# Forming the combine products of a mixture-of-experts layer among the first experts instead of in the output stage

## The chip, the cores and the metric

One core of one Trainium2 chip runs the kernel. The metric is the device time of one execution in microseconds (us). The kernel before takes 350.67 us, the median of three runs (350.11 to 351.55).

## What is computed

Causal attention over 2 batches, 12 heads, 448 positions and head size 64 gives x, 896 tokens of 768 numbers. Two layers follow, cut here to what matters:

```python
logits = x @ phi                       # 32 slots
slot_input = softmax(logits, 0).T @ x  # 8 experts of 4 slots
slot_out[e] = relu(slot_input[e] @ w1[e]) @ w2[e]
c = softmax(logits, 1)                 # combine weights, 896 x 32
y = c @ slot_out                       # never formed by the kernel
out = ((y @ w_a) * (y @ w_b)) @ w_out  # d_ff = 1536
```

With A = slot_out @ w_a and B = slot_out @ w_b (32 rows each), the product (y @ w_a) * (y @ w_b) is a sum over pairs of slots (i, j) of c_i c_j times A_i B_j. So the kernel forms two things for each of the 528 pairs of slots: the products c_i c_j for every token (called cc here), and the rows M = (A_i B_j + A_j B_i) @ w_out. The output is cc times M. The pairs are cut into five blocks, k = 0 to 4; blocks 0 to 3 hold 128 pairs, the last one 16.

## The kernel before, in words

The kernel issues every instruction in an order written out by hand (`manual_schedule`): each engine works its own list from the front, and waits there.

Attention fills the first 120 us. Meanwhile `w_a`, `w_b` and `w_out` arrive as packed halves (the `raw` tiles, 0 to 35, 768 KB each) and are turned into floats by `conv_begin` and `conv_step` (two ACT passes L174 and L177, one DVE pass L218). Raw 32 to 35 are the last four parts of `w_out`.

Then come the eight experts, whose weights stream through SyncE's queue as 64 tiles w0 to w63 of 768 KB, in the order of use. `order` (L456 to L480) gives each transfer its place and its home, one of the slots r0 to r3, q0 to q3, t0 to t3; `pump` (L486) issues transfers from the front of that list as long as the next one's slot is free, and stops at the first that is not. After the first two rounds over twelve slots (`HOMES`) the homes repeat over six slots, r0 to r3, q0 and q1 (`ring6`): a tile is then requested when the tile six places earlier has been used. `rsel`, a 320 KB table of zeros and ones that picks pairs of slots, is loaded after w31 (`NSEL`), and raw 32 to 35 stand after w21, w31, w32 and w33 (`RPOS`).

`group` runs the experts in `GROUPS` (0 to 3, then 4 and 5, then 6 and 7): for each expert `exp_h` (four tiles of first-layer weights, lines L682), `exp_hp`, and `exp_so` (four tiles of second-layer weights, L723). Between tiles `spare()` takes units of other work, as many as the table `BG` tells. In the first group these are the units that turn the softmax of the logits into `cst`, the transposed combine weights in two parts (`combine_units`: `cw_max`, `cw_copy`, `cw_turn`). In experts 2 and 3 (`KEEPE`) each tile is preceded by five small matmuls whose result nobody reads (`keep`, L354). In groups 1 and 2 the spare units are a `Stage`: `fold_a`, `fold_b`, `ab_chunk` (A and B of the slots just done, L809), `ab_turn`, the products A_i B_j on DVE (`products`, L891 to L903; `p_tile`, L922 and L923), the splitting of `w_out` into a high and a low part (`w_split`, ACT L947 then DVE L948, into `wtm` in slots t2, t3, and q0, q1 at the end), and the matmuls `m_mats` (L953) that give M for block 0 or 1.

The last stage (from 264 us) computes A and B for the last group (`half_chunk`, L839), M for blocks 2, 3 and 4 (`m_late`, L953), splits the remaining `w_out` (`w_late`), and forms cc. Its units sit in the gaps between PE's blocks (`gap`, with the table `TAIL`). Each `cc_step(n, k)` (L1111) takes 256 tokens and two of the five blocks: up to four selection matmuls pick c_i and c_j (L1134, two PSUM tiles), ACT copies the one (L1138), DVE multiplies by the other (L1139), ACT rounds the product to the high part (L1142), and POOL subtracts to get the low part (L1143). The narrow last block takes L1147 and L1149. `o_mats` (L1246, L1253) multiplies cc by M for 128 tokens at a time, and `o_store` evicts and stores.

Of the kernel before, what the change touches and what calls it, by code (L numbers as in the profile page):

```python
# [21 lines left out]
S = 448  # L22
# [7 lines left out]
for _i in range(7):  # L30
# [42 lines left out]
BG = {  # L73
# [24 lines left out]
KEEPE = (2, 3)  # L98
# [5 lines left out]
def moe_kernel(ctx: ExitStack, tc: tile.TileContext, pk, vt, phi, w1, w2, wab, wo, rsel, out):  # L104
# [16 lines left out]
    ident16 = const.tile([128, 128], BF16, name="ident16")  # L121
# [26 lines left out]
    phi_sb = const.tile([128, NPAIR, NSLOT], F32, name="phi_sb")  # L148
# [203 lines left out]
    def keep(ps, n):  # L352
        for _ in range(n):
            nc.tensor.matmul(  # L354
                ps, lhsT=ident16[:, 0:ps.shape[0]], rhs=ident16[:, 0:ps.shape[1]], start=True, stop=True,
                skip_group_check=True,
            )
# [97 lines left out]
    ring6 = ["r0", "r1", "r2", "r3", "q0", "q1"]  # L455
# [60 lines left out]
    def arrive(k):  # L516
        while cursor[0] < pos["w", k]:
# [3 lines left out]
            elif kind == "rsel":  # L521
                rr = slot_tile("q3", F32R, "rs")[0:64, 0:1280]
                nc.scalar.activation(out=rr, in_=rin[0], func=AF.Copy)
                mq[1] = rr.rearrange("p (k q j) -> p k q j", k=5, q=2)
                freed.add(("rsel", 0))
# [6 lines left out]
    with tc.manual_schedule():  # L532
# [216 lines left out]
        cst = r2.tile([64, 2, S], F32R, name="cst")  # L749
# [42 lines left out]

        def combine_units():
# [569 lines left out]
```

## Time and profile before

| | |
|---|---|
| median of three runs | 350.67 us |
| profiled execution, its own time | 351.46 us |
| its span, first to last instruction | 349.40 us |
| PE busy | 329.3 us (94%) |
| DVE busy | 207.8 us (59%) |
| ACT busy | 184.7 us (53%) |
| POOL busy | 83.7 us (24%) |
| DMA, mean over the span | 259 GB/s |

Busy is the time in which an engine ran an instruction. All times in the rows below are us from the start of the span. The profiled execution is 0.8 us above the median, 0.2%.

### The profile page before, as it was taken

How to read it: one execution, taken by the hardware profiler on the slowest of the kernel's cores; microseconds unless marked ns; L12 is line 12 of the kernel's file. 1: busy time of each engine (PE TensorE's matmuls, PEld its weight loads, DVE VectorE, ACT ScalarE, POOL GpSimd, SP SyncE). 2: the span in 40 equal slices, each digit the busy share in tenths (PEclk: the TensorE clock that was granted, in tenths of full speed). 3: DMA queues.
4: the chain of work that ended last, by engine and by line, in shares of the span. 5: the costliest groups of instructions: out<-in, count | busy, mean ns of one | idle time of the engine just before them, and what ended most of it. 6: DMA issues, size and time to landing. Idle time of an engine off the chain costs nothing.

```text
span 349.4 us, 7132 instructions
## 1 busy us (share of the span) xinstructions
PE 329.3 (94%) x2695; PEld 209.2 (60%) x2695; DVE 207.8 (59%) x587; ACT 184.7 (53%) x419; POOL 83.7 (24%) x150
## 2 busy tenths in 40 slices
PE   7999899999999989889988699998999999999996
PEld 5566556655656744433432357434565589989895
DVE  4799889979899640210034976408855899523221
ACT  2799989999899510131038344414445542543321
POOL 2566677765575300010000000000000000121210
PEclk9999999999999999999989989999999999999999
DMA  7799998998998889999999989779910000002122
GB/s 271 312 337 336 357 337 256 374 386 316 386 345 293 277 357 347 421 416 413 402 310 398 419 270 358 253 280 312 421 80 2 1 3 0 2 0 90 55 82 90
DMA packets 20225, 90.53 MB, mean 259 GB/s; under 512 B 2336, under 2 KB 5024, under 8 KB 20192
## 3 DMA queue, kind: packets, MB, share of 16 engines
q1 hardware_dynamic: 20192, 90.09, 69.2%
q8 instruction: 21, 0.34, 0.4%
q14 instruction: 12, 0.10, 0.1%
HBM read 87.33 MB, written 2.75 MB: 258 GB/s over the span
## 4 chain that ended last, share of the span: by engine, by line
PE 72%; DVE 12%; DMA 8%; ACT 4%; issue 1%; POOL 1%; SPq 1%; ACTq 0%; DVEq 0%; POOLq 0%
PE M L953 12%; PE s L277 10%; PE o L1253 9%; PE v L371 7%; PE t L335 6%; PE h L682 5%; PE so L723 5%; DMA qk<-in_pk_dram 4%; DMA raw<-in_wo_dram 4%; PE ab L809 3%; DVE pf L892 2%; DVE pt L891 2%; PE c L1134 2%; PE hp L702 2%; DVE pf L903 2%; PE xt L384 1%
## 5 line engine op out<-in xcount | busy, mean ns | idle before, releaser
L322 POOL TENSOR_SCALAR p<-p,rc 128x448 f32<-128x448 f32 (+6 forms) x84 | 59.0, 718 | 10.9 <-DVE rc L319 10.2
L277 PE MATMUL s<-qk 64*64 64x448 f32 (+6 forms) x336 | 47.2, 394 | 1.6 <-POOL qk L258 1.1
L1143 POOL TENSOR_TENSOR cc<-gt,cc 128x512 fp32r<-128x512 f32 (+1 forms) x6 | 6.6, 1101 | 165.3 <-ACT cc L1142 165.3
L298 ACT ACTIVATE p<-s,nm 128x448 f32<-128x448 f32 (+6 forms) x84 | 39.7, 484 | 8.9 <-DVE nm L288 8.2
L953 PE MATMUL M<-wt,P_t 128*128 128x384 f32 x168 | 35.7, 355 | 3.0 <-DVE wt L948 1.0
L953 PEld LDWEIGHTS M<-wt,P_t 128*128 128x128 f32 x168 | 29.2, 193 | 12.2 <-ACT wt L947 4.8
L283 DVE TENSOR_REDUCE nm<-s 128x1 f32<-128x448 f32 (+6 forms) x84 | 31.8, 413 | 6.2 <-PE s L277 6.2
L277 PEld LDWEIGHTS s<-qk 64*64 64x64 f32 x336 | 19.6, 133 | 22.0 <-issue 15.0
L682 PE MATMUL h<-w,sT 128*32 128x512 f32 x192 | 29.9, 613 | 2.1 <-ACT hs L695 1.6
L335 PE MATMUL t<-ident,p 128*128 128x128 f32 x192 | 31.1, 286 | 0.0
L948 DVE TENSOR_TENSOR wt<-wo,wt 128x384 fp32r<-128x384 f32 x48 | 23.8, 551 | 10.4 <-ACT wt L947 10.4
L947 ACT ACTIVATE wt<-wo 128x384 fp32r<-128x384 f32 x48 | 21.8, 513 | 13.6 <-PE M L953 13.1
L371 PE MATMUL v<-pT,v 128*64 128x192 f32 (+2 forms) x336 | 27.4, 299 | 0.0
L335 PEld LDWEIGHTS t<-ident,p 128*128 128x128 f32 x192 | 20.1, 141 | 11.4 <-issue 7.1
L723 PE MATMUL so<-w,hpad 128*32 128x384 f32 x256 | 24.8, 493 | 1.3 <-DMA w<-in_w_dram 0.6
L174 ACT ACTIVATE wab<-raw,shr 128x768 f32<-128x768 int8 x24 | 24.6, 1025 | 1.0 <-DMA raw<-in_wab_dram 1.0
L218 DVE SCALAR_TENSOR_TENSOR wab<-raw,wab 128x768 uint32<-128x768 uint32 x24 | 24.0, 1001 | 1.0 <-ACT wab L177 0.9
L177 ACT ACTIVATE wab<-wab,shr 128x768 int32<-128x768 f32 x24 | 22.9, 952 | 0.0
L371 PEld LDWEIGHTS v<-pT,v 128*64 128x64 f32 (+1 forms) x336 | 19.2, 135 | 6.0 <-issue 2.8
L1139 DVE TENSOR_TENSOR gt<-gt,c 128x512 f32<-128x512 f32 (+2 forms) x12 | 6.5, 544 | 25.7 <-ACT gt L1138 25.7
L809 PE MATMUL ab<-wab,sT 128*32 128x384 f32 x192 | 20.0, 523 | 0.5 <-DVE sT L647 0.5
L174 ACT ACTIVATE wo<-raw,shr 128x768 f32<-128x768 int8 x12 | 12.4, 1032 | 14.9 <-DMA raw<-in_wo_dram 14.9
(164 smaller groups left out, 533.5 us busy)
## 6 DMA issues: line engine op xcount, KB each, us to landing
w<-in_w_dram SPq DMA_DIRECT2D x64, 768.0 KB, 8.6
raw<-in_wab_dram SPq DMA_DIRECT2D x24, 768.0 KB, 6.7
raw<-in_wo_dram SPq DMA_DIRECT2D x12, 768.0 KB, 6.8
qk<-in_pk_dram SPq DMA_DIRECT2D x12, 448.0 KB, 6.2
v<-in_pk_dram SPq DMA_DIRECT2D x12, 192.0 KB, 6.3
out_dram<-ost SPq DMA_DIRECT2D x6, 384.0 KB, 2.3
v<-in_vt_dram SPq DMA_DIRECT2D x12, 32.0 KB, 6.1
out_dram<-ost SPq DMA_DIRECT2D x2, 192.0 KB, 1.9
```

The source lines that it names most:

```text
L174: nc.scalar.activation(out=dst, in_=top, func=AF.Prelu, bias=shr[:, 0:1], scale=1.0, alpha=2.0 ** -40)
L277: nc.tensor.matmul(sb[r, o:o + n], lhsT=qT[r, 64 * i:64 * i + 64], rhs=kT[r, 0:n], start=False, stop=True, skip_group_check=True,)
L283: nc.vector.tensor_reduce(out=d["nm"][:, c:c + 1], in_=sb[:, o:o + 64 * (i + 1)], axis=AX.X, op=ALU.max, negate=True)
L298: nc.scalar.activation(out=d["p"][:, POFF[i]:POFF[i] + n], in_=sb[:, o:o + n], func=AF.Exp, bias=d["nm"][:, c:c + 1], scale=d["scale"], ac ...
L322: nc.gpsimd.tensor_scalar(out=p[:, POFF[i]:POFF[i] + n], in0=p[:, POFF[i]:POFF[i] + n], scalar1=rc[:, CIX[i]:CIX[i] + 1], scalar2=1.0, op0 ...
L335: nc.tensor.transpose(ps[:, j, :], d["p"][:, o:o + 128], ident)
L371: nc.tensor.matmul(ps[r, 64 * i:64 * (i + n)], lhsT=v[k, kt, h, :], rhs=d["pT"][k, b0:b0 + by * (n - 1) + 1:by, r], start=(kt == 0), stop= ...
L682: nc.tensor.matmul(ps[32 * g:32 * g + 32, :], lhsT=sT[:, 0, c, :], rhs=wt[8 * e + i // 3][:, 512 * (i % 3):512 * (i % 3) + 512], start=(i ...
L723: nc.tensor.matmul(so[32 * g:32 * g + 32, 0:384], lhsT=t[:, c, :], rhs=wt[8 * e + 4 + i // 4][:, 384 * (i % 4):384 * (i % 4) + 384], start ...
L809: nc.tensor.matmul(abps[q][32 * g:32 * g + 32, 0:384], lhsT=sT[:, 1, c, :], rhs=w[:, c % 2, 384 * g:384 * g + 384], start=(c == 0), stop=( ...
L953: nc.tensor.matmul(mps[k][h][:, 0:384], lhsT=l[:, f, :], rhs=r, start=(n == 0 and i == 0), stop=(n == 11 and i == 2))
L1253: nc.tensor.matmul(ops[t][h][:, 0:384], lhsT=hl[k // 2][:, l, k % 2, o], rhs=mhl[k][:, r, 384 * h:384 * h + 384], start=(k == 0 and i == 0 ...
```

## The change

The selection matmuls, the ACT copy and the DVE product move from the last stage into the first group of experts, as ten new units `cc_make(n, k)` at the end of `combine_units`. They work on 512 tokens (n = 0) or 384 (n = 1) and one block k each, so there are 20 matmuls in place of 40. The products wait in memory: in slots q1 and q3 and in the places of the logits (`lsb`), of `phi` and of the softmax (`cs`). In the last stage `cc_split(n, k)` only rounds the high part (ACT) and subtracts for the low part (DVE, where POOL did it).

To make room, q1 and q3 leave the rotation after one use and q2 after one use and `rs`; `HOMES` has nine slots in its later rounds, and the steady ring has five (r0 to r3, q0). `rsel` comes after w11 in three transfers, is converted by three ACT copies as the first spare unit (`rs_cast`), and raw 32 moves to after w31. Two of the last stage's split parts of `w_out` move to later gaps and other slots (`w_late`, `TAIL["W"]`), the filler matmuls in experts 2 and 3 are gone (`KEEPE = ()`), and the scratch of block 4 moves from `lsb` to the place of `cst`.

```diff
-RPOS = (21, 31, 32, 33)
-NSEL = 31
+RPOS = (31,31,32,33)
+NSEL = 11
 HOMES = (
-    "r0", "r1", "r2", "r3", "q0", "q1", "q2", "q3", "t0", "t1", "t2", "t3", "r0", "r1", "r2", "r3", "q0", "q1",
-    "q2", "q3", "t0", "t1", "t2", "t3",
+    "r0", "r1", "r2", "r3", "q0", "q1", "q2", "q3", "t0", "t1", "t2", "t3", "r0", "r1", "r2", "r3", "q0", "t0", "t1", "t2", "t3", "r0", "r1", "r2", "r3", "q0", "t0", "t1", "t2", "t3",
 )
-NQ = 62
+NQ = 60
 BG = {
-    "B": ((0, 0, 0, 0, 0, 0, 0, 0, 0, 0, 0, 1, 0, 3, 0, 3, 3, 1, 0, 2), ...
+    "B": ((0, 0, 0, 0, 0, 0, 0, 0, 1, 1, 0, 0, 0, 1, 0, 1, 3, 1, 2, 1, 1, 0, 1, 1, 1, 0, 1, 1, 1, 0, 1, 1, 1, 0, 1), ...
 TAIL = {
-    "W": {2: 2, 3: 2, 4: 4, 13: 2, 14: 2, 15: 2, 16: 2},
+    "W": {2: 2, 3: 2, 4: 2, 13: 2, 14: 2, 15: 2, 16: 2, 18: 2},
-    "C": {36: 1, 39: 1, 41: 1, 43: 1, 46: 1, 49: 1, 53: 1, 56: 1, 59: 1, 62: 1, 65: 1, 68: 1},
+    "C": {30: 1, 32: 1, 34: 1, 36: 1, 38: 1, 40: 1, 42: 1, 44: 1, 46: 1, 48: 1},
-KEEPE = (2, 3)
+KEEPE = ()
...
-    ring6 = ["r0", "r1", "r2", "r3", "q0", "q1"]
+    steady = ["r0", "r1", "r2", "r3", "q0"]
...
-                home = ring6[nb % 6]
+                home = steady[nb % 5]
...
-                rin.append(slot_tile(s, F32, "rin")[0:64, 0:1280])
-                nc.sync.dma_start(out=rin[0], in_=rsel)
+                r2 = r2box["q"]
+                rin.append(r2.tile([128, 768], F32, tag="abt", bufs=1, name="rin0")[0:64])
+                for i in range(2):
+                    rin.append(r2.tile([128, 384], F32, tag="pt", bufs=2, name=f"rin{i + 1}")[0:64, 0:256])
+                for i in range(3):
+                    nc.sync.dma_start(out=rin[i], in_=rsel[:, (0, 768, 1024)[i]:(768, 1024, 1280)[i]])
...
+        def cc_make(n, k):
+            if not gs:
+                g_homes()
+            t0 = 512 * n
+            w = (512, 384)[n]
+            cstf = cst.rearrange("p b t -> p (b t)")
+            ab = []
+            for q in range(2):
+                ps = psM.tile([128, 512], F32, tag="m", name=f"c{q}_{n}_{k}")
+                ab.append(ps[:, 0:w])
+                nc.tensor.matmul(ab[q], lhsT=mq[1][:, k, q, :], rhs=cstf[:, t0:t0 + w], start=True, stop=True)
+            for i, g in enumerate(gs[n, k] if isinstance(gs[n, k], list) else [gs[n, k]]):
+                x = slice(256 * i, 256 * i + g.shape[-1])
+                nc.scalar.activation(out=g, in_=ab[0][:, x], func=AF.Copy)
+                nc.vector.tensor_tensor(out=g, in0=g, in1=ab[1][:, x], op=ALU.mult)
+
+        def rs_cast():
+            rr = slot_tile("q2", F32R, "rs")[0:64, 0:1280]
+            for i in range(3):
+                nc.scalar.activation(out=rr[:, (0, 768, 1024)[i]:(768, 1024, 1280)[i]], in_=rin[i], func=AF.Copy)
+            mq[1] = rr.rearrange("p (k q j) -> p k q j", k=5, q=2)
+
         def combine_units():
-            q = [cw_max, lambda: (cw_copy(0), cw_copy(1))]
+            q = [rs_cast, cw_max, lambda: (cw_copy(0), cw_copy(1))]
             for i in range(8):
                 q.append(lambda i=i: (cw_turn(i), i < 6 and cw_copy(i + 2)))
+            q += [lambda n=n, k=k: cc_make(n, k) for n in range(2) for k in range(5)]
...
-                    name = f"q{f - 8}" if self.k == len(STAGES) - 1 and f in (8, 9) else f"t{2 + f % 2}"
+                    name = {8: "q0", 11: "r0"}.get(f) if self.k == len(STAGES) - 1 else None
+                    name = name or f"t{2 + f % 2}"
...
         def late_next():
-            if wl_j[0] < (8 if nchunk[0] < 2 else 12 if nchunk[0] < 4 else 16):
+            if wl_j[0] < (6 if nchunk[0] < 2 else 10 if nchunk[0] < 4 else 16):
...
+        def cc_split(n, k):
+            if (n, k) in ((0, 0), (1, 2)):
+                cc_homes(n)
+            if k < 4:
+                h, l = ccv[n, k]
+                g = gs[n, k]
                 nc.scalar.activation(out=h, in_=g, func=AF.Copy)
-                nc.gpsimd.tensor_tensor(
-                    out=hl[k][:, 1, :, 0:w], in0=g, in1=h.bitcast(F32), op=ALU.subtract
-                )
+                nc.vector.tensor_tensor(out=l, in0=g, in1=h.bitcast(F32), op=ALU.subtract)
+                return
```

## Rows read from the trace of the kernel before

**Rows 1.** Windows: stretch, length, busy us (instructions) by engine, PEclk, DMA share, GB/s
```profile
132.60:164.70 32.10, 29.02 (x263) 12.45 (x263) 3.81 (x12) 5.51 (x10) 1.91 (x9) 1.00 1.01 415
175.30:200.00 24.70, 19.97 (x157) 8.02 (x153) 13.93 (x56) 13.63 (x22) 0.00 (x0) 0.93 1.01 378
307.00:346.00 39.00, 38.91 (x214) 35.26 (x212) 11.33 (x23) 12.89 (x28) 7.21 (x7) 1.00 0.17 66
```
**Rows 2.** Chain of waits from 296.0 to the end (53.4 us): shares, one piece
```profile
by line: PE o L1253 58.1%; PE M L953 17.7%; PE c L1134 12.8%; PE o L1246 5.0%; ACT ost L1266 0.9%; issue 0.1%; ACTq L1266 0.1%
...
303.79 0.67 PE c L1134 x4
```
**Rows 3.** Timeline of one cc step: start, us, engine, line, [idle before]
```profile
313.98 0.60 ACT L1138 ACTIVATE gt<-c 128x512 f32<-128x512 f32 x1 [2.01 <-PE c L1134]
...
314.61 0.69 DVE L1139 TENSOR_TENSOR gt<-gt,c 128x512 f32<-128x512 f32 x1 [3.30 <-ACT gt L1138]
...
315.33 0.64 ACT L1142 ACTIVATE cc<-gt 128x512 fp32r<-128x512 f32 x1 [0.75 <-DVE gt L1139]
...
316.04 1.28 POOL L1143 TENSOR_TENSOR cc<-gt,cc 128x512 fp32r<-128x512 f32 x1 [2.71 <-ACT cc L1142]
```
**Rows 4.** PE's timeline around expert 2's first tile and the last tile of expert 3
```profile
157.85 0.45 PE L354 MATMUL idle<-ident 128*128 128x128 bf16 x5
158.23 1.06 PE L682 MATMUL h<-w,sT 128*32 128x512 f32 x6
...
174.50 0.85 PE L723 MATMUL so<-w,hpad 128*32 128x384 f32 x8 [0.61 <-DMA w<-in_w_dram]
```
**Rows 5.** Transfers by tile, one issue each: rsel, then w32
```profile
L501 SPq DMA_DIRECT2D rin<-in_rsel_dram x1: 472/472/472, 166.8 to 166.8; - x1
...
DMA to landing us min/median/max: 13.3/13.3/13.3
...
L505 SPq DMA_DIRECT2D w<-in_w_dram x1: 334/334/334, 169.1 to 169.1; - x1
...
DMA to landing us min/median/max: 12.6/12.6/12.6
```
**Rows 6.** Windows (columns as Rows 1) around two transfers' stretches and two low-clock stretches
```profile
130.50:133.00 2.50, 2.08 (x25) 1.48 (x26) 1.03 (x3) 0.00 (x0) 0.00 (x0) 1.00 0.49 88
...
173.60:179.60 6.00, 4.26 (x35) 1.81 (x37) 1.87 (x3) 1.76 (x2) 0.00 (x0) 0.79 1.03 246
...
177.03:180.44 3.41, 3.07 (x20) 0.99 (x24) 1.86 (x3) 2.18 (x3) 0.00 (x0) 0.50 1.00 290
200.92:204.33 3.41, 3.41 (x11) 1.75 (x12) 3.06 (x14) 0.94 (x2) 0.00 (x0) 0.50 0.73 221
```
**Rows 7.** ACT's timeline: conversion of raw 34 at the start of group 1
```profile
183.62 1.04 ACT L174 ACTIVATE wo<-raw,shr 128x768 f32<-128x768 int8 x1 [2.14 <-DMA raw<-in_wo_dram]
```
**Rows 8.** Transfers issued at 235.2 and 236.7 (w55 and w56 of the kernel before)
```profile
L505 SPq DMA_DIRECT2D w<-in_w_dram x1: 328/328/328, 235.2 to 235.2; - x1
...
DMA to landing us min/median/max: 4.5/4.5/4.5
...
L505 SPq DMA_DIRECT2D w<-in_w_dram x1: 327/327/327, 236.7 to 236.7; - x1
...
DMA to landing us min/median/max: 6.8/6.8/6.8
```
**Rows 9.** PE's and DVE's timelines in expert 7 and stage 1
```profile
238.17 2.78 PE L682 MATMUL h<-w,sT 128*32 128x512 f32 x24 [0.70 <-ACT hs L695]
...
244.57 1.69 PE L723 MATMUL so<-w,hpad 128*32 128x384 f32 x16 [0.43 <-ACT wt L947]
...
246.44 1.96 DVE L948 TENSOR_TENSOR wt<-wo,wt 128x384 fp32r<-128x384 f32 x4
```
**Rows 10.** DVE's timeline before block 2's second products, and PE's wait for them
```profile
277.16 3.89 DVE L948 TENSOR_TENSOR whl<-wo,whl 128x384 fp32r<-128x384 f32 x8
...
284.83 3.22 PE L953 MATMUL M<-whl,P_t 128*128 128x384 f32 x17 [0.32 <-DVE P_t L923]
```

More of the change, by code (lines that the diff above doesn't have):

```diff
@@ L354, in keep @@
             nc.tensor.matmul(
-                ps, lhsT=ident16[:, 0:ps.shape[0]], rhs=ident16[:, 0:ps.shape[1]], start=True, stop=True,
-                skip_group_check=True,
+                ps, lhsT=ident.bitcast(BF16)[:, 0:ps.shape[0]], rhs=ident.bitcast(BF16)[:, 0:ps.shape[1]],
+                start=True, stop=True, skip_group_check=True,
             )
@@ L469, in moe_kernel @@
             if kind == "rsel":
-                order.append((kind, 0, "t2"))
+                order.append((kind, 0, "-"))
                 continue
@@ L489, in pump @@
             x, s = order[0][:2], order[0][2]
-            if s in holder and holder[s] not in freed:
+            if s == "-" and r2box.get("q") is None or s in holder and holder[s] not in freed and s != "-":
                 return
@@ L520, in arrive @@
                 conv_to(i)
[L521 to L525, printed above, removed]
             cursor[0] += 1
@@ L747, in group @@
                 spare()
-        cst = r2.tile([64, 2, S], F32R, name="cst")
+        cst = r2.tile([128, 2, S], F32R, tag="cst", bufs=1, name="cst")[0:64]
         cw = {}
@@ L1017, in p4_make @@
         def p4_make():
-            mx["p"] = const.tile([128, 12, 32], F32, tag="lsb", name="p4")
+            mx["p"] = r2.tile([128, 12, 32], F32, tag="cst", bufs=1, name="p4")
             nc.gpsimd.memset(mx["p"][:, :, 16:32], 0.0)
@@ L1033, in m4_copy @@
         def m4_copy():
-            mx["c"] = const.tile([128, 768], F32, tag="lsb", name="mc")
+            mx["c"] = r2.tile([128, 768], F32, tag="cst", bufs=1, name="mc")
             for h in range(2):
@@ L1076, in moe_kernel @@
                 mq[0] = slot_tile("q2", F32, "mq")
+                abl.append(r2.tile([128, 12, 2, NSLOT], F32, tag="abt", bufs=1, name="abt"))
+                av += [abl[0][:, :, q, :] for q in range(2)]
             if gi:
@@ new lines, in moe_kernel, with cc_homes @@
+        ccv = {}
+        def cc_homes(n):
+            if n == 0:
+                t3 = wabp.tile([128, 3, 2, 512], F32R, tag="wab3", bufs=1, name="cc3")
+                t4 = wabp.tile([128, 3072], F32R, tag="wab4", bufs=1, name="cc4")
+                for k in range(3):
+                    ccv[0, k] = t3[:, k, 0], t3[:, k, 1]
+                ccv[0, 3] = t4[:, 0:512], t4[:, 512:1024]
+                ccv[0, 4] = t4[:, 1024:1536],
+                for k in range(2):
+                    ccv[1, k] = [t4[:, 1536 + 768 * k + 384 * i:1920 + 768 * k + 384 * i] for i in range(2)]
+            else:
+                t = [slot_tile(j, F32R, f"cc{j}") for j in ("t0", "t1")]
+                for k in range(2):
+                    ccv[1, 2 + k] = [t[k][:, 384 * i:384 * i + 384] for i in range(2)]
+                ccv[1, 4] = t[0][:, 768:1152],
@@ L1148, in cc_step @@
                 q = slice(64, 96)
-                nc.vector.tensor_tensor(
-                    out=last[q, 0:w], in0=g[q, 0], in1=last[q, 0:w].bitcast(F32), op=ALU.subtract
-                )
+                nc.vector.tensor_tensor(out=last[q, x], in0=g[q], in1=last[q, x].bitcast(F32), op=ALU.subtract)
         mhl = {}
@@ L1169, in m_split @@
                 )
-        ccq = [(n, k) for n in range(4) for k in range(3)]
+        ccq = [(n, k) for n in range(2) for k in range(5)]
         ptq = {2: [0], 3: [0]}
@@ L1186, in cc_next @@
         def cc_next():
-            if len(turned) > 1 and ccq and (ccq[0][0] == 0 or done3 or ccq[0][0] == 1):
-                cc_step(*ccq.pop(0))
+            if ccq and (nchunk[0] > 3 if ccq[0] < (1, 2) else done):
+                cc_split(*ccq.pop(0))
         spot = [0]
-        done3 = []
+        done = []
         splits = [2, 0, 1]
@@ L1233, in o_mats @@
         def o_mats(t, k, hs=(0, 1)):
-            while ccq and ccq[0][0] <= t // 2:
+            while ccq and ccq[0] <= (t // 4, k):
                 cc_next()
@@ L1274, in moe_kernel @@
             gap()
+        done.append(2)
         for i in range(12):
@@ L1277, in moe_kernel @@
             gap()
-        done3.append(1)
         while splits:
```

82 lines of the change are left out of this document (32 added, 50 removed), and 2 rows, old and new, of the table BG.

## Prediction

> **What bounds the kernel now.** I read the windows by stretch first. From 307 to 346 us PE is busy 38.91 of 39.00 us, with ACT, DVE and POOL far from full [rows 1], so in the last stage each instruction taken off PE shortens the run by its own length. The chain of waits says the same: of its last 53.4 us, 12.8% are the selection matmuls L1134 [rows 2], 6.84 us, and no piece of it belongs to ACT, DVE or POOL before the last eviction. The same windows show another regime among the first experts: from 132.6 to 164.7 us the DMA engines are taken whole (share 1.01, 415 GB/s), and they stay so until 200 us [rows 1]. A tile of 768 KB takes 1.9 us there (786 KB / 415 GB/s). PE arrives at the last tile of expert 3 at 174.5 and waits 0.61 us for it [rows 4]; where the transfers set the pace, work put on PE costs nothing while it stays below that pace. So the change moves work from a stage that PE bounds into one that the transfers bound, and the questions are how much returns through the slots and transfers that it moves as well.
>
> **The last stage.** Forty selection matmuls leave PE. Four of 256 columns are 0.67 us in the chain [rows 2], and all forty are the 6.84 us above, their switching included. The ACT copy (0.60 us) and the DVE product (0.69) go too [rows 3]. What remains per block is a rounding on ACT (0.64 for 512 numbers per partition) and the subtraction, now on DVE at about the 0.69 of its other 512-wide operation, instead of 1.28 on POOL [rows 3]. In the gaps from the 30th on (M for block 3 is running) DVE gets ten such subtractions, some 6 us, and loses 7.6 us of products and narrow parts, so it is no later than before. A gain of 6.84, hidden by nothing.
>
> One edit costs here. In `TAIL["W"]` two of eight split parts move from gap 4 to later gaps, and two end in gap 18, just ahead of block 2's second set of products. DVE's splits run without a break there, eight in 3.89 us, 0.49 each [rows 10], and ACT's half stands ahead of the eviction that the products need. The products start about 1.0 us later, and PE already waits 0.32 us for them at 284.83 [rows 10]; that wait has no cover, so it grows by 1.0 (bounds 0 and 1.2). Last stage: -6.84 + 1.0 = -5.8 us.
>
> **Experts 0 to 3.** PE loses 16 sets of five fillers. A set occupies 157.85 to 158.23 [rows 4], 0.38 us, so 6.1 us go. It gains 20 selection matmuls. By the 0.17 us of one with 256 columns [rows 2], scaled by columns from that upwards, one of 384 is 0.19 to 0.25 and one of 512 is 0.21 to 0.34; I take 0.19 and 0.24, as the chain grows little with the columns elsewhere, 4.3 us in all. Each pair then waits for two PSUM tiles to be read (0.60 + 0.69 us [rows 3]), and h tiles of 0.99 us lie between, so the waits are some tenths each. The new first unit `rs_cast` takes slot q2, which holds w6 until expert 0's third second-layer tile; ACT therefore stands until then, and the softmax of the combine weights, queued behind it on ACT, comes about 1 us later. I count 0.4 us of new waits for the turns. In sum PE needs about 1 us less in this group than before; as it waited for the transfers at the end, the transfers decide.
>
> Transfers: raw 32 no longer stands ahead of w31, -1.9 us. rsel now does. Its cost is read at its old place: w31 was there at 174.5 [rows 4], w32 landed at 169.1 + 12.6 = 181.7 [rows 5], and raw 33, rsel and w32 lie between; two tiles are 3.8 us, so rsel took 3.4, far over the 0.8 that 328 KB cost at full rate. The rate shows it: 246 GB/s from 173.6 to 179.6 [rows 6]. At its new place the engines are half idle (share 0.49 from 130.5 to 133.0 [rows 6]), which absorbs 1.3 us. So w31 lands at 174.5 - 1.9 + 3.4 - 1.3 = 174.7, no change; with rsel at 0.8 it would be 172.6, with 5 (three smaller transfers in place of one, an estimate from the 3.4) 176.3. Behind w31 the idle 1.3 us that were filled remain as a gain: w32, w33 and raw 34 come 1.3 us earlier. Raw 34 matters: ACT waits 2.14 us for it at 183.62 [rows 7], and its conversion stands ahead of the splits and the eviction from which stage 0's products start. PE cannot take all of it; I count -0.5 us at 200 us (bounds -2.5 and +1.5).
>
> **The ring of five.** A tile is now requested when the tile five places before it is used, so w(n) gets the request time that w(n+1) had. Following PE's order of use through groups 1 and 2, I find one place where that is too late, expert 7: the long block of A and B matmuls ahead of it frees no slot, so its last tiles are requested late. Before, w55 was issued at 235.2 and landed 4.5 us later, at 239.7, just in time; w56, issued at 236.7, landed after 6.8 us, at 243.5 [rows 8]. Now w54 and w55 get those two requests. Expert 7's first layer starts at 238.17 and takes 2.78 us for w52 to w55 [rows 9], so it needs w55 at 239.9 and has it at 243.5: PE stops for 3.4 to 3.6 us. The value for a full-rate queue would be 1.9 us after w54, 241.6, a stop of 1.6; the row at that very place says 3.5, and I take it.
>
> Part of the stop is absorbed: DVE is the late engine there, with products and splits to 248.4 [rows 9], and PE waits for it several times (0.43 at 244.57 [rows 9], three more of the kind). Following the slots t2 and t3 of the splits, which are freed by PE, I find block 1's fifth part of twelve done 1.8 us later than before.
>
> A stop this long also tends to cost clock. The granted clock was 0.50 from 177.03 to 180.44 and from 200.92 to 204.33 [rows 6], its lower level of 1.2 GHz; each time PE had just had several waits of 0.5 to 0.9 us. With such a spell after the stop PE loses up to half of 3.41 us, 1.7; part lies in the stop, so 1.2, and the fifth part comes 3.0 us later in all. The Trainium skill, "TensorE: Matmul & The Clock Gate", section "HAM oscillation", says that waits for a DMA between bursts of matmuls throw the clock to its half; by that rule fewer slots and no fillers are the wrong direction. The two spells agree with it. Nothing in the sum needs the sentence.
>
> The splits that go to t3, t2 and r0 instead of q1, t2 and t3 wait for tiles used 1 to 3 us before the split is needed: nothing. The other moves (scratch of block 4, `ident` for the fillers) cost nothing.
>
> **Sum.** -5.8 (last stage) + 3.0 (expert 7) - 0.5 (groups 0 and 1) = -3.3 us on the profiled span of 349.40, which gives 346.1. The profiled execution took 351.46, 0.8 above the median; I put the difference on the median of 350.67: 347.4.
>
> **Rivals.**
> - The stop is cheap: w55 lands at the full-rate spacing, or DVE's lateness hides it, and the clock stays. Then expert 7 costs 0 to 1.8, and the result is 344.3 to 346.2, centre 345.3. For it: DVE is busy 3.9 us of work past the stop. Against: the request times are those of rows 8.
> - The change does not do what it says on balance: the middle takes back what the end gives. rsel at 5 us (+1.6), the stop unabsorbed (+3.5 and 1.2 for the clock) against -5.8 give 351.2 at most, centre 350.2.
> - Slower: the clock falls in experts 2 and 3, where the fillers stood, and stays down. Selection matmuls now come only between tiles, and PE waits for `cst` shortly before. At the lower level six matmuls of a tile take 1.8 instead of 0.99 us, so each us there costs half a us of work, and the transfers no longer cover it, as PE has nearly no lead at w31. It decides from about 11 us of lower clock: 5.5 us of loss exceed the 3.3 of gain by more than 0.5%. All 17 us would give 347.4 + 8.5 = 356. By the Trainium skill's rule on that page this is the way it would go. Against: PE has no idle time between the tiles there, and the spells of this trace ended after 3.4 us.
>
> **Chances.** Forecast 0.45 (346 to 348.8), cheap stop 0.25, gain given back 0.18, slower 0.12. A difference of 0.5%, 1.75 us, is about what a measurement of this kernel can tell from no change. The first two cases lie below 348.9 nearly whole; from the third, a little is faster too: faster 0.71, same 0.18, slower 0.11. For 8 times in 10 the range reaches from the cheap stop with cheap rsel (344.0) to the gain given back (350.6).
>
> **What would show it.** The profile of the changed kernel should have no selection matmuls after 264 us, and some 6 us less PE time from 284 to the end; PE's wait for P at block 2 should be about 1.3 us. In expert 7's first layer a wait for a DMA of 3.4 us on its last tile should stand, with granted clock 0.50 behind it; its absence is the first rival. The window of experts 2 and 3 should be at clock 1.00 and end within 1 us of 175.4; if it does not, rsel or the clock is why. The prediction fails if the tail's other engines, not PE, turn out to be late, or if other tiles of the ring come late as well.

## The result, and the profile after

The changed kernel takes 348.07 us, the median of 20 executions, beside 350.13 for 20 of the kernel before. A second set of runs gave 346.97 (six executions) against 350.40. By these medians it is faster by 0.6 and 1.0%, where 347.4 us, 0.9% less, was forecast. The ratios are 0.9886 (95% interval 0.9859 to 0.9914) and 0.9865 (0.9815 to 0.9916); they and the ratios below leave out executions more than 1.5% above the fastest of their kernel, which are 9 of the 20 and 1 of the 6 here and none of the kernel before, and so show more gain than the medians do. Its times scatter far more (343.6 to 356.7 us) than those of the kernel before (348.2 to 353.3); the reason stands below, under the slower rival.

The forecast sum, -3.3 us, is near what the medians show (-2.1 and -3.4 us). Its terms aren't: the end of the kernel gives 2.3 us more than forecast, and expert 7 takes 2.6 us more. Two executions of the changed kernel were profiled; the rows below are of the second (span 345.3 us), unless said otherwise.

The windows that answer to [rows 1]: stretch, length, busy us (instructions) of PE, weight loads, DVE, ACT and POOL, then PEclk (the granted clock: the share of TensorE's full clock that it was given), DMA share, GB/s:

```profile
132.60:164.70 32.10, 29.73 (x241) 12.06 (x243) 6.25 (x16) 7.59 (x15) 1.77 (x8) 1.00 1.01 402
175.30:200.00 24.70, 20.43 (x174) 9.16 (x166) 15.54 (x61) 14.77 (x25) 0.26 (x1) 1.00 0.94 360
307.00:342.00 35.00, 34.77 (x199) 34.44 (x198) 9.03 (x18) 5.82 (x14) 0.00 (x0) 1.00 0.19 74
```

In the last window PE is still busy nearly throughout, and POOL has nothing left to do. The chain of waits from 296 us on, by line and its first pieces, answers to [rows 2]: no selection matmul stands in it, and M and o follow each other unbroken.

```profile
by line: PE o L1281 58.8%; PE M L988 28.1%; PE o L1274 4.9%; ACT ost L1294 1.0%; issue 0.1%; ACTq L1294 0.1%
...
295.86 14.07 PE M L988 x81
309.93 7.28 PE o L1281 x42
```

The two waits that the prediction added stand in PE's timeline (start, us, line, operation, count, and in brackets the idle time before it and what ended it). The first row is expert 7's last tile, w55, which answers to [rows 9]; its request, at 235.0, landed 7.5 us later, where [rows 8] had 6.8. The last row is block 2's wait for its products, which answers to [rows 10].

```profile
236.48 2.85 PE L680 MATMUL h<-w,sT 128*32 128x512 f32 x18 [0.70 <-ACT hs L693]
242.53 1.85 PE L680 MATMUL h<-w,sT 128*32 128x512 f32 x6 [3.19 <-DMA w<-in_w_dram]
244.31 1.88 PE L700 MATMUL hp<-sel,hs 128*128 128x8 f32 x8
246.04 3.91 PE L988 MATMUL M<-wt,P_t 128*128 128x384 f32 x12
...
289.70 3.28 PE L988 MATMUL M<-whl,P_t 128*128 128x384 f32 x17 [1.10 <-DVE P_t L958]
```

The six matmuls of a tile take 1.85 us there and not 1.06, twelve M matmuls 3.91 and not 2.34: this is the lower clock level, 1.2 GHz (PEclk 0.50). The window of that spell, from 242.70 on, has PE busy in all of its 6.83 us:

```profile
242.70:249.53 6.83, 6.83 (x25) 5.22 (x20) 2.75 (x15) 1.62 (x4) 0.00 (x0) 0.50 0.97 402
```

**Where the time went.** The start and end of the h and so matmuls in PE's timeline cut every trace into the same stretches. They repeat to 0.1 us wherever the clock is up and no wait differs, so one trace of each kernel says more about a stretch than its times do. The table has all kernels that follow; "spells" are the stretches of granted clock 0.50 up to PE's end.

| kernel | experts 0-3 | to expert 4 | experts 4, 5 | h of 6 and 7 | to the end of so 7 | to PE's end | spells |
|---|---|---|---|---|---|---|---|
| before | 42.8 | 7.4 | 40.6 | 16.1 | 21.3 | 83.7 | 177.0-180.4, 200.9-204.3 |
| changed, first trace | 45.2 | 8.9 | 39.1 | 21.5 | 21.6 | 75.6 | 171.2-184.9, 201.9-205.4, 246.3-253.1 |
| changed, second trace | 44.1 | 6.0 | 38.3 | 21.2 | 21.8 | 75.6 | 171.0-174.4, 242.7-249.5 |
| before_ring5 | 42.9 | 6.1 | 41.5 | 19.6 | 22.4 | 83.7 | 198.5-201.9, 242.8-249.7 |
| before_ring5fill | 42.8 | 7.6 | 40.4 | 20.6 | 19.4 | 83.7 | 176.8-180.2, 200.7-204.1 |
| before_nofill | 42.7 | 7.5 | 38.7 | 16.1 | 21.3 | 83.7 | 152.1-155.6, 165.8-172.6, 176.0-179.4 |
| after_fill | 51.0 | 6.0 | 38.3 | 20.3 | 22.3 | 75.6 | 152.0-155.4, 175.9-179.3, 247.6-254.4 |
| after_stopfill | 46.0 | 8.0 | 38.3 | 20.7 | 19.4 | 75.6 | 169.8-183.4 |
| after_spread | 43.8 | 6.0 | 38.3 | 16.8 | 24.2 | 75.5 | 142.0-145.4, 244.4-247.8 |
| after_w24 | 42.6 | 6.0 | 38.5 | 19.8 | 22.5 | 74.6 | 239.3-246.2 |
| after_sel40 | 42.6 | 6.0 | 39.0 | 21.2 | 21.6 | 85.4 | 239.6-246.4 |
| after_sel40one | 45.0 | 6.0 | 38.3 | 21.0 | 21.9 | 81.4 | 150.8-154.2, 171.3-174.7, 242.9-249.8 |
| best | 45.0 | 9.2 | 39.3 | 16.8 | 22.3 | 74.6 | 170.6-184.3, 201.3-204.7 |
| best_fill3 | 46.9 | 6.0 | 39.4 | 16.8 | 23.6 | 74.6 | 169.7-176.5, 200.4-203.9, 251.6-255.1 |

From before to the second trace: the last stretch gives 8.1 us; experts 6 and 7 take 5.1 and 0.5; experts 0 to 3 with the way to expert 4 are level (50.2 and 50.1); experts 4 and 5 give 2.3, of which 1.8 answers to a low-clock spell at 200.9 that the kernel before had in this execution (before_nofill, without one there, has 38.7). The stretch ahead of expert 0, which the table leaves out, differs by 0.7.

### The profile page after: what moved, and what is told of

Its sections match the earlier page's. It is cut to its first block, busy times and chain, and to the rows that moved or that the text cites. A ratio compares the mean times of both kernels' runs of the same rounds, so it can differ in the third digit from the quotient of the medians.

```text
span 349.3 us, 6930 instructions
## 1 busy us (share of the span) xinstructions
PE 328.2 (94%) x2595; PEld 207.5 (59%) x2595; DVE 210.7 (60%) x593; ACT 183.0 (52%) x419; POOL 74.3 (21%) x142
## 4 chain that ended last, share of the span: by engine, by line
PE 69%; DVE 11%; DMA 8%; ACT 6%; issue 3%; POOL 3%; POOLq 0%; ACTq 0%; DVEq 0%
PE M L988 13%; PE o L1281 8%; PE s L276 7%; PE h L680 6%; PE ab L844 5%; PE v L370 5%; PE t L334 5%; PE so L721 5%; DMA w<-in_w_dram 3%; DMA raw<-in_wab_dram 3%; PE hp L700 2%; DMA qk<-in_pk_dram 2%; PE c L815 2%; POOL p L321 1%; DVE pf L927 1%
## 5 line engine op out<-in xcount | busy, mean ns | idle before, releaser
L321 POOL TENSOR_SCALAR p<-p,rc 128x448 f32<-128x448 f32 (+6 forms) x84 | 58.3, 710 | 10.7 <-DVE rc L318 10.0
L988 PE MATMUL M<-wt,P_t 128*128 128x384 f32 x168 | 36.5, 365 | 2.2 <-ACT wt L982 0.9
L988 PEld LDWEIGHTS M<-wt,P_t 128*128 128x128 f32 x168 | 30.4, 200 | 10.6 <-ACT wt L982 5.8
L680 PE MATMUL h<-w,sT 128*32 128x512 f32 x192 | 31.5, 624 | 5.2 <-DMA w<-in_w_dram 3.5
L276 PEld LDWEIGHTS s<-qk 64*64 64x64 f32 x336 | 19.7, 134 | 21.6 <-issue 15.5
L982 ACT ACTIVATE wt<-wo 128x384 fp32r<-128x384 f32 x48 | 21.9, 513 | 16.0 <-PE M L988 15.8
L721 PE MATMUL so<-w,hpad 128*32 128x384 f32 x256 | 27.0, 527 | 0.6 <-ACT hpad L708 0.3
L217 DVE SCALAR_TENSOR_TENSOR wab<-raw,wab 128x768 uint32<-128x768 uint32 x24 | 22.8, 948 | 0.7 <-ACT wab L176 0.7
L844 PE MATMUL ab<-wab,sT 128*32 128x384 f32 x192 | 20.6, 541 | 0.4 <-DVE sT L645 0.4
L926 DVE TENSOR_TENSOR pt<-abt 128x192 f32<-128x192 f32 (+16 forms) x80 | 18.3, 229 | 4.3 <-ACT abt L886 3.7
L927 DVE TENSOR_TENSOR pf<-abt 128x12 f32<-128x12 f32 (+19 forms) x95 | 19.5, 219 | 0.0
L297 ACT ACTIVATION_READ_ACCUMULATOR p<-s,nm 128x1 f32 x84 | 18.2, 217 | 0.0
```

What stands on the lines that cost most here:

```text
L276: nc.tensor.matmul(sb[r, o:o + n], lhsT=qT[r, 64 * i:64 * i + 64], rhs=kT[r, 0:n], start=False, stop=True, skip_group_check=True,)
L297: nc.scalar.activation(out=d["p"][:, POFF[i]:POFF[i] + n], in_=sb[:, o:o + n], func=AF.Exp, bias=d["nm"][:, c:c + 1], scale=d["scale"], ac ...
L321: nc.gpsimd.tensor_scalar(out=p[:, POFF[i]:POFF[i] + n], in0=p[:, POFF[i]:POFF[i] + n], scalar1=rc[:, CIX[i]:CIX[i] + 1], scalar2=1.0, op0 ...
L680: nc.tensor.matmul(ps[32 * g:32 * g + 32, :], lhsT=sT[:, 0, c, :], rhs=wt[8 * e + i // 3][:, 512 * (i % 3):512 * (i % 3) + 512], start=(i ...
L721: nc.tensor.matmul(so[32 * g:32 * g + 32, 0:384], lhsT=t[:, c, :], rhs=wt[8 * e + 4 + i // 4][:, 384 * (i % 4):384 * (i % 4) + 384], start ...
L844: nc.tensor.matmul(abps[q][32 * g:32 * g + 32, 0:384], lhsT=sT[:, 1, c, :], rhs=w[:, c % 2, 384 * g:384 * g + 384], start=(c == 0), stop=( ...
```

## The experiments

**The changed kernel again.** No edit.

> The changed kernel once more, for a second trace of it. Every theory expects 346 to 350 us, against 350.1 of the kernel before. The theory that the stop at tile w55 and the low clock behind it belong to the ring of five expects both again: about 3.5 us of idle ahead of the last h matmuls of expert 7, and a granted clock of about 0.5 behind them. The theory that the spell of low clock at 171 to 185 us in the first trace came from leaving the fill matmuls of experts 2 and 3 out expects it again at the same place; if it moves or is absent, that spell is chance of the one execution.

346.97 us. The stop in expert 7 and the spell behind it are in both traces. The 13.65 us spell at 171 us isn't: the second trace has one of 3.4 us there. So the first belongs to the kernel and the second to single executions.

**The ring of five alone, in the kernel before.**

```diff
-NQ = 62
+NQ = 60
...
-    ring6 = ["r0", "r1", "r2", "r3", "q0", "q1"]
+    ring6 = ["r0", "r1", "r2", "r3", "q0"]
...
-                home = ring6[nb % 6]
+                home = ring6[nb % 5]
```

> The kernel before with the weight tiles going round five homes instead of six (q1 left out) and nothing else. The theory of the prediction (the ring of five makes w55 late, the stop costs its length less what later waits absorb, and the low clock behind it costs about 1.2) expects a wait of 2.5 to 4.5 us at w55 in expert 7, and 2 to 4 us more in the end time. The rival (a late tile there is hidden, since the following stage waits for other things anyway) expects the same wait with less than 1 us in the end time. A third: the tile isn't late in the kernel before, because its transfers lie otherwise; then no wait and no difference.

355.07 us, ratio 1.0140 (1.0095 to 1.0186), 4.7 us more than before, over the upper end of the first theory. The timeline of PE and the window of the spell:

```profile
241.97 1.10 PE L682 MATMUL h<-w,sT 128*32 128x512 f32 x6 [2.42 <-DMA w<-in_w_dram]
243.00 1.88 PE L702 MATMUL hp<-sel,hs 128*128 128x8 f32 x8
244.73 4.19 PE L953 MATMUL M<-wt,P_t 128*128 128x384 f32 x12
...
242.85:249.68 6.83, 6.83 (x31) 5.80 (x32) 3.47 (x16) 2.35 (x6) 0.00 (x0) 0.50 1.00 415
```

The stretch of the h matmuls grows from 16.1 to 19.6, which is 3.5, the size of the stop that was forecast; the stretch behind it grows by another 1.1. The rival of a hidden stop falls. But how much of the 1.1 is clock, and how much was absorbed, this run doesn't tell.

**The same, with fill matmuls in the stop.** Forty matmuls that nobody reads stand ahead of w55's.

```diff
+                    if e == 7 and i == 9:
+                        keep(psA.tile([128, 512], F32, tag="mm1", name=f"idle7_{i}")[:, 0:128], 40)
```

> The kernel before with the ring of five and 40 fill matmuls, read by nobody, ahead of w55 in expert 7, where PE waits. The stop (3.5 us from expert 6's first h to expert 7's last) should stay. If the low clock behind it costs 2.5 to 3 us and the queue ahead of ACT and DVE takes up 1.8 us of the stop, the stretch behind it goes from 22.4 to 19.5 us, under the 21.3 of the kernel before, and the whole ends some 1.7 us later than that instead of 4.7. If the clock costs 1.2 us and nothing is taken up, the stretch goes to 21.2.

352.95 us, ratio 1.0064 (1.0037 to 1.0091). The timeline of PE, and a window behind the stop:

```profile
240.33 2.41 PE L354 MATMUL idle<-ident 128*128 128x128 bf16 x40
243.86 1.06 PE L684 MATMUL h<-w,sT 128*32 128x512 f32 x6 [1.13 <-DMA w<-in_w_dram]
244.85 1.06 PE L704 MATMUL hp<-sel,hs 128*128 128x8 f32 x8
245.77 2.34 PE L955 MATMUL M<-wt,P_t 128*128 128x384 f32 x12
...
244.85:252.88 8.03, 8.03 (x58) 6.40 (x55) 5.60 (x17) 5.27 (x12) 0.00 (x0) 1.00 1.02 407
```

The windows of the whole stretch from the last h matmul to the end of so 7, without the fill matmuls and with them:

```profile
243.07:265.51 22.44, 22.15 (x141) 16.21 (x141) 13.04 (x36) 10.57 (x24) 0.00 (x0) 0.85 0.62 234
...
244.92:264.32 19.40, 19.11 (x142) 13.62 (x141) 12.03 (x31) 10.57 (x24) 0.00 (x0) 1.00 0.65 247
```

The clock stays at 1.00, and the stretch behind takes 19.4 us, as expected by the first theory. Against the 22.4 without them that is 3.0 us less, all of it busy time of PE. Against the 21.3 of the kernel before, the stop takes up 1.9 us: DVE and ACT run ahead while PE stands, and the waits for them that [rows 9] shows don't come.

For the ring alone both figures are upper bounds, since the stop did not stay as it was. The tile came 1.0 us later in this execution: it landed 7.7 us after its request and not 6.6, PE waits 1.13 us even behind the fill matmuls, and the h matmuls take 20.6 us and not 19.6. If that last microsecond was wholly taken up as well, the clock costs 2.0 us and the ring's own stop is covered by 0.9. The medians differ by 2.1 us.

**The same in the changed kernel.** Twenty fill matmuls ahead of w54's, forty ahead of w55's, otherwise as above.

> The changed kernel with 20 and 40 fill matmuls, read by nobody, ahead of the last two h tiles of expert 7 (w54 and w55), in the 4.7 us in which PE waits there. The theory that the clock falls because PE idles expects the spell of half clock behind the stop gone and 0.5 to 1.5 us less in the end time, the waits themselves unchanged. The rival, that the spell comes from something else, expects the spell to stay and no change, or up to 1 us more where the fill matmuls last longer than the waits.

345.72 us, ratio 0.9820 (0.9778 to 0.9863). The spell behind the stop is gone, and the stretch takes 19.4 us against 21.6 and 21.8:

```profile
242.00:250.00 8.00, 8.00 (x82) 5.74 (x84) 6.05 (x28) 2.47 (x6) 0.00 (x0) 1.00 1.01 404
```

These 2.2 to 2.4 us are more than the 0.5 to 1.5 expected, and the h matmuls ahead take 0.5 to 0.7 us less, as w55's six run at full clock. The medians differ by 1.3 and 2.4 us; this execution had the long spell at 170 us.

**The stop removed by order alone.** The block of 14 units (the A and B transforms) that stands behind expert 6's first tile is dealt out, so that its second and third tile are read, and their homes freed, some 6 us earlier.

```diff
-(2, 14, 2, 0, 0, 0, 0, 0, 2, 0, 3, ...)   # "B", group 2
+(2, 2, 2, 12, 0, 0, 0, 0, 2, 0, 3, ...)
-(1, 0, 1, 0, 4, 0, 0, 1, 1, 7, ...)       # "P", group 2
+(1, 0, 0, 0, 5, 0, 0, 1, 1, 7, ...)
```

> The changed kernel with the 16 units of stage work of experts 6 and 7 dealt out otherwise: 2, 2, 2 and 12 of them behind the first four stops of that group, instead of 2, 14, 2 and 0; the five product steps that followed the first turn go behind expert 6's last tile. Nothing is added or removed; tiles 49 and 50 are read some 6 us earlier, so the homes that w54 and w55 wait for come free earlier. The theory that the ring of five is short only because three read-later tiles hold their homes through that block of 14 units expects the waits at w54 and w55 (4.7 us together) and the low clock behind them gone: 4 to 5.7 us less, 341 to 343 us. The rival, that the transforms that now end 2 us later make the products and so expert 7's M matmuls late, expects 1 to 3 us of that given back as a wait on DVE. The theory that DMA throughput, not the homes, makes the tiles late expects no change.

347.05 us, ratio 0.9823 (0.9780 to 0.9867). The waits for w54 and w55 are gone (16.8 us for the h matmuls, the 24 of expert 7 in one piece), which refutes that the queue's throughput alone makes them late. But 2.4 us of the gain come back in the next stretch, so that experts 6 and 7 take 2.0 us less than in the second trace (41.0 against 43.0) and not 4 to 5.7. The medians differ by at most 1.0 us. The timeline of PE, then of DVE:

```profile
235.50 2.78 PE L680 MATMUL h<-w,sT 128*32 128x512 f32 x24 [0.71 <-ACT hs L693]
238.21 1.06 PE L700 MATMUL hp<-sel,hs 128*128 128x8 f32 x8
239.13 2.34 PE L988 MATMUL M<-wt,P_t 128*128 128x384 f32 x12
244.83 1.51 PE L721 MATMUL so<-w,hpad 128*32 128x384 f32 x8 [3.37 <-ACT wt L982]
...
244.13 0.56 DVE L938 TENSOR_TENSOR pf<-pf,pt 128x384 f32<-128x384 f32 x1
244.65 0.09 DVE L705 MEMSET hpad<- 128x32 f32 x1
```

The trace puts the wait down to ACT's `wt`, which isn't what `so` reads: it reads `hpad`, and the clearing of `hpad` (0.09 us on DVE) stood behind the fourth product of the stage and came at 244.65. The rival was right in its size and in DVE, not in what was queued there. A spell of 3.4 us at the lower clock begins at the end of this wait (244.4 to 247.8), though it is a wait for DVE and not for a transfer.

**The fill matmuls of experts 2 and 3, taken out of the kernel before.** `KEEPE = ()`.

> The kernel before without the fill matmuls of experts 2 and 3 and nothing else. The theory that they only hold the clock expects a granted clock that falls to about 0.5 somewhere between 157 and 185 us, and 0 to 4 us more in the end time. The prediction's step, that transfers decide this stretch and the fill matmuls fill PE's waits for them, expects within 1 us. The theory that PE is the bound expects up to 6.1 us less, the sum of their durations.

350.77 us, ratio 1.0020 (0.9996 to 1.0045): no difference. Experts 0 to 3 take 42.7 and 42.8 us, although 10.2 us of them are at the lower clock, in spells of 3.4 and 6.8 us (window of the longer one):

```profile
165.80:172.60 6.80, 6.52 (x40) 2.77 (x38) 0.19 (x1) 0.00 (x0) 0.00 (x0) 0.50 1.02 419
```

So in the kernel before the transfers decide this group, as predicted, and cover fill matmuls and low clock alike. The equal time doesn't refute the first theory, that the fill matmuls hold the clock: with them none of the three traces of this kind (before, before_ring5, before_ring5fill) has a spell in these experts.

**The same fill matmuls put back into the changed kernel.** `KEEPE = (2, 3)`.

> The changed kernel with the fill matmuls in experts 2 and 3 back, 80 to 120 matmuls that nobody reads. The theory that they hold the clock up expects the low spell at 171 to 185 us (13.65 us at half speed in the first trace, 4 to 7 us of lost matmul time) gone or shortened, and, since PE ended group 0 there and not the transfers, 2 to 5 us less in the end time. The rival, that PE is the bound of that stretch and each fill matmul costs its duration, expects 2 to 6 us more. The prediction's own step, that DMA decides the stretch, expects within 1 us.

351.27 us, ratio to before 1.0016 (0.9979 to 1.0052), 4.3 us more than the second set without them; experts 0 to 3 take 51.0 us. The timeline of PE has each set at its full price of 0.38 us, beside the pairs of selection matmuls:

```profile
160.44 0.73 PE L815 MATMUL c<-cst,rs 64*128 64x512 f32 x2
161.10 0.45 PE L353 MATMUL idle<-ident 128*128 128x128 bf16 x5
161.48 1.06 PE L680 MATMUL h<-w,sT 128*32 128x512 f32 x6
162.47 0.73 PE L815 MATMUL c<-cst,rs 64*128 64x512 f32 x2
163.14 0.45 PE L353 MATMUL idle<-ident 128*128 128x128 bf16 x5
```

PE is the bound of this group now, the rival, and the prediction's "DMA decides" is refuted. No wait for a transfer is left on PE from 131 to 182 us in this trace, nor in that of after_w24. Two spells of 3.4 us are in this group all the same.

**The two splits moved behind the products.** `"W": {..., 18: 2}` becomes `24: 2`.

> The changed kernel with the two w_out splits of gap 18 moved to gap 24, behind the products of block 2. The prediction's step (these splits stand on DVE ahead of the product that M waits for) expects the wait of M for P_t, 1.1 us in both traces, back to 0.3 to 0.5 and 0.6 to 1.0 us less from the last expert to PE's end (75.6 us in both traces). The rival, that DVE's products are the bound there whatever stands between, expects the same wait; a second, that the moved splits are then late for the matmuls that read them, expects a new wait on ACT or DVE of about the same size.

344.04 us (four executions), ratio 0.9805 (0.9755 to 0.9854). The last stretch goes from 75.6 to 74.6 us, the wait is what it was before, and no new wait comes in its place:

```profile
284.57 3.23 PE L988 MATMUL M<-whl,P_t 128*128 128x384 f32 x17 [0.31 <-DVE P_t L958]
```

**What forty selection matmuls cost in the last stage.** Unread ones of 64 partitions and 256 columns, in ten blocks of four, with no work of other engines:

```diff
+    "D": {36: 1, 39: 1, 41: 1, 43: 1, 46: 1, 49: 1, 53: 1, 56: 1, 59: 1, 62: 1},
...
+                    nc.tensor.matmul(
+                        ps[:, c, :], lhsT=mhl[0][0:64, c, 0:128], rhs=mhl[0][0:64, 0, 0:256], start=True, stop=True,
...
+                    )
```

> The changed kernel with 40 selection-like matmuls that nobody reads (64 partitions, 256 columns) put back into the last stage in ten blocks of four, where the kernel before had its twelve blocks; no work of ACT, DVE or POOL with them. The prediction priced the forty by the durations in the chain, which is 6.7 us here: then the stretch from the last expert's last matmul to PE's end goes from 75.6 to 82.3 us. The theory that every switch from a stream of M or o matmuls to another and back costs 0.1 to 0.2 us more than the chain's pieces show expects 83.3 to 84.3. If it stays under 82.3, the rest of the 8.1 us that the stretch got shorter by is work of the other engines.

355.29 us, ratio 1.0122 (1.0067 to 1.0176). The last stretch takes 85.4 us, 9.8 more, over what each theory gave; 1.1 of that is a wait of the first block for its own operand, seen as the gap between its first two matmuls. So 8.7 us, against 6.7 by the durations in the chain and 7.7 to 8.7 with dear switches. The timeline shows where the rest is:

```profile
309.95 0.74 PE L1237 MATMUL d<-ml 64*128 64x256 f32 x4
310.62 2.35 PE L1291 MATMUL o<-ml,cc 128*128 128x384 f32 x12
312.91 0.74 PE L1237 MATMUL d<-ml 64*128 64x256 f32 x4
313.58 1.31 PE L1291 MATMUL o<-mhl,cc 128*128 128x384 f32 x6
314.73 2.25 PE L1291 MATMUL o<-ml,cc 128*128 128x384 f32 x12
316.90 0.74 PE L1237 MATMUL d<-ml 64*128 64x256 f32 x4
```

A block takes 0.67 us from its start to the next row's. But the twelve o matmuls from 310.62 to 312.91, between two blocks, take 2.29 us, and twelve in the changed kernel without blocks 2.08: a further 0.21 us that the chain books on o.

**The same forty in one block.** `"D": {49: 10}`.

> The changed kernel with the same 40 unread selection-like matmuls in the last stage, all in one block instead of ten. If the surplus over their durations (9.8 us measured with ten blocks, of which 0.9 was a wait for ml, against 6.7) belongs to the switches between streams, the last stretch goes from 75.6 to 82.2 to 82.8 us; if it belongs to each matmul, to 84.5.

353.17 us in its one execution; the last stretch takes 81.4, 5.8 more:

```profile
317.63 5.75 PE L1237 MATMUL d<-ml 64*128 64x256 f32 x40
323.31 1.31 PE L1291 MATMUL o<-mhl,cc 128*128 128x384 f32 x6
```

That is less than every theory gave: 0.14 us for one in a stream of its like. Ten blocks cost 2.9 us more than one (8.7 less 5.8), so each of the nine further blocks costs 0.3 us for its switches, of which 0.1 lies in the block's own 0.67 us and 0.2 behind or ahead of it.

**Three orders altered together.** The units as in after_spread; "P" of group 2 as (1, 0, 0, 0, 2, 0, 0, 0, 2, 7, ...), so that `hpad` is cleared behind one product; the splits as in after_w24.

> The changed kernel with three orders altered and nothing added: the stage units of experts 6 and 7 dealt 2, 2, 2, 12 as before, the products of that stage dealt so that only one stands on DVE ahead of the clearing of hpad (in the earlier version three did, and the so matmuls waited 3.4 us) and the w_out splits of the second pair stand ahead of the third product, and the two w_out splits of gap 18 moved to gap 24. If the three waits (w54 and w55, hpad, P_t) were each worth what their stages showed, the stretch from expert 6 to the last expert's end falls from 43.0 to 37 to 39 us and the last stretch from 75.6 to 74.6: 5 to 6 us below the changed kernel, 340 to 342 us. If the DVE queue of that stage is the bound whatever the order, the first gain is 2 us and the sum 3.

In after_spread it was four products that stood ahead of `hpad`, not three.

345.04 us, ratio 0.9816 (0.9767 to 0.9864). The two stretches behind expert 5 and the last one are as hoped (39.1 and 74.6 us, 3.8 and 1.0 under the second trace of the changed kernel; `so` no longer waits for `hpad`, a wait of 1.7 us for the third w_out split is left). The median is 2 to 3 us under the changed kernel's, not 5 or 6. In this execution the rest is lost early: experts 0 to 3 and the way to expert 4 took 54.1 us, for the clock was at its lower level from 170.60 to 184.30.

```profile
170.60:184.30 13.70, 12.48 (x70) 4.47 (x66) 6.89 (x12) 8.34 (x13) 0.26 (x1) 0.50 0.95 387
```

It beats the kernel before clearly. That it beats the changed kernel is shown by the stretches; the intervals of the times overlap.

**Sixteen fill matmuls in expert 3, in that version.** `KEEPE = (3,)`, `KEEPW = 2`.

> The same with 16 fill matmuls, two ahead of each tile of expert 3, read by nobody (some 1 us of PE). The theory that the long low-clock spell of some executions at 170 to 184 us comes from the fill matmuls that are missing there expects it not to be seen and a median some 1 us lower with less spread; the rival, that it has another cause, or that so few don't matter, expects the median 0 to 1 us higher.

346.09 us, ratio 0.9864 (0.9819 to 0.9909), and a spell of 6.8 us from 169.7 on in spite of them. The missing fill matmuls aren't the cause of the spells there, or so few don't matter; in either case they are no remedy.

## Why the prediction was right in sum, and where its terms were wrong

| term | forecast | measured | from |
|---|---|---|---|
| forty selection matmuls gone | -6.8 | -9.1 | 83.7 to 74.6 (before and after_w24, both with a P wait of 0.3) |
| w_out splits ahead of the products | +1.0 | +1.0 | 75.6 to 74.6 |
| stop in expert 7 | +3.5 | +3.5 ring alone; +5.1 to 5.4 changed kernel, of which 0.8 to 0.9 is w55's matmuls at the lower clock | 16.1 to 19.6, 21.2, 21.5 |
| of it absorbed | -1.7 (3.5 less the 1.8 that it let through) | -0.9 to -1.9 ring alone; -1.9 changed kernel | 21.3 to 19.4, clock up, stop 1.0 longer than in the ring alone |
| low clock behind the stop | +1.2 | +2.0 to 3.0 ring alone; +2.2 to 2.4 changed kernel, besides the 0.8 to 0.9 above | 22.4, 21.6 and 21.8, all to 19.4 |
| experts 0 to 3 and the way to expert 4 | -0.5 | -1.7 to +3.9, by the clock | 50.2 to 48.5 (after_w24) or 54.1 (first trace) |

**The last stage** was a question of PE alone, as read from [rows 1] and [rows 2]. The failed step is "all forty are the 6.84 us above, their switching included". The chain books a switch partly on the neighbours: the c pieces hold 0.67 us, the o and M pieces behind them the rest. Twelve blocks left; by after_sel40 and after_sel40one a block's switches cost 0.3 us and a matmul 0.14, which makes 9.4 for the twelve blocks and forty matmuls, where 9.1 was measured. The Trainium skill says, under "Back-to-back issue gap" on the page "TensorE: Matmul & The Clock Gate", that the spacing in a stream of loads and matmuls is set by both, pipelined. Whether that is why the same matmul takes 0.14 us in one block and 0.22 in blocks of four, no run here shows. The step on the splits was right: with them gone from there, the wait falls by 0.8 us and the stretch by 1.0.

**Expert 7.** The reading of the slots, the two requests of [rows 8] and the stop of 3.4 to 3.6 us were right for the ring alone, and what DVE's lateness absorbs is not far off (0.9 to 1.9, where 1.7 was forecast). Two sizes failed. The spell behind the stop was put at 3.41 us, as the two of [rows 6], with part of it inside the stop; it was 6.83 us in every trace that has the stop and no fill matmuls in it, and no more than 0.4 us of it lies in the stop. That is "1.2" where 2.0 to 3.0 belonged. And in the changed kernel w55 lands 0.7 to 0.9 us later than [rows 8], and in both of its traces the six matmuls run at the lower clock already (1.85 and 1.93 for 1.06). The first rival, a cheap stop, is refuted in both its forms. The second had the loss here better (3.5 and 1.2 make 4.7, where experts 6 and 7 took 5.6), and fails by the larger gain at the end. The rule of "HAM oscillation" on the same page of the Trainium skill, that waits for a transfer between bursts of matmuls throw the clock to its half, holds here: behind the wait for w55 the clock is at 0.50 in all seven traces that leave PE idle in it, and at 1.00 in the two that feed PE through it. The two spells of [rows 6] bear it out less than the prediction said: of the waits just ahead of them one was for a transfer (0.61 us), the others for DVE and ACT (0.68; 0.94 and 0.83).

**Experts 0 to 3.** That the transfers decide was true of the kernel before (before_nofill) and untrue of the changed one (after_fill). The mis-sized term is the selection pairs: ten of them take 0.54 to 0.79 us from start to start in after_w24, 6.6 us together where 4.3 were counted, and PE still waits 0.3 to 0.6 us at a time for ACT, DVE and POOL around the turns and the first pair. So PE needs as long as the group took before, 42.6 us without a spell, and the transfers, with w31 landing 0.7 us (after_w24) to 3.1 us (second trace) ahead of its use, no longer hide anything. rsel cost about what was read from [rows 5], 3.2 us in the spacing of the landings around it in the second trace, and delayed nobody. The group was to end within 1 us of 175.4; it ends at 173.7 without a spell (after_w24) and at 177.4 and 177.6 with the spells of the changed kernel's two traces, so the clock, and not rsel, is why.

**The slower rival** came true in some executions, and near its price of half a us for each us. A spell of 13.65 us begins in expert 3, at 170 to 171 us, and lasts past the group's end, in three of the ten traces of the changed kernel and those made from it, in none of the four of the other kind. Such an execution takes 54.0 to 54.2 us to expert 4, against 48.5 without a spell: 5.6 us, which more than takes the gain back. The executions without a trace tell the same. For each the mean granted clock was noted. As the levels are 0.50 and 1.00, twice what this mean lacks of 1, times the span, is the time at the lower level (10.4 us for the second trace, whose two spells sum to 10.2). The 26 executions of the changed kernel spent 6.8 to 34.8 us there, 23 of the kernel before 0 to 10.5. In the changed kernel the time rises by 0.42 us for each us of it (correlation 0.96), in the kernel before by 0.07 (0.18). So this is the scatter of the result: the transfers cover the lower clock in the kernel before and no longer do in the changed one.

On the rival's reason, the missing fill matmuls, the runs say two things. The 12 executions of the kernel before without them spent 10.4 to 17.5 us at the lower clock (mean 13.8), the 23 with them 0 to 10.5 (mean 5.0), and took no longer. So there they do hold the clock. But back in the changed kernel, eighty of them cost more than they save, and sixteen left a spell of 6.8 us. Why the clock falls there in some executions and not in others stays open.

So the sum held because two errors nearly cancel: 2.3 us too little gain at the end, and 2.6 too little loss in expert 7 (42.97 us from expert 6's first h to the end of so 7 in the second trace, 37.35 before, where 3.0 more were forecast). That is luck, and so is part of the median's place, for the sum has 1.2 us for the clock, and the clock alone moves single executions by several times that.

## What to carry to other kernels

Price a block of foreign matmuls in a stream by what the stream takes with and without it, start to start across several blocks, not by the block's own pieces in the chain. A stop of PE costs its length, less what late engines catch up in it, plus the clock behind it, and this last term was 2 to 3 us behind stops of 2.4 to 3.5: take the stop away by freeing the slot earlier, or keep PE fed through it. When work is moved to where transfers hide it, ask how much more than that work they can hide: here they hid fill matmuls and clock spells, and with the moved work they hid neither, so that the time came to follow the clock.

## What the runs showed of the hardware

- Selection matmuls of 256 columns take 0.14 us each in a block of forty, 0.17 in blocks of four by their own pieces, and 0.22 with all that the switches cost their neighbours.
- After the stop of 2.4 to 3.5 us at w55 the granted clock was 0.50 for 6.83 us in seven of seven traces, with PE busy in all but the first 0.4 us at most, twice the spells of [rows 6]. Behind a stop of 3.37 us for DVE (after_spread) it was 3.41 us. 40 unread matmuls of 128 columns (2.41 us in all) in the stop kept it at 1.00, in two of two.
- Programs that are the same up to expert 3 run through it with no spell (after_w24), with one of 3.4 us, or with one of 13.7 (the two traces of the changed kernel).
- Each us at the lower clock costs 0.42 us in the changed kernel, where PE sets the pace nearly throughout, and 0.07 in the kernel before; there 10.2 us of it in experts 0 to 3 (before_nofill) leave them at 42.7 us, against 42.8 with none.
